# Two output banks with a longer scheduled lag, a second transpose bank in the drain, and every sixth gate multiplication on GpSimd, in a scan followed by a mixture of adapters

## Chip, cores, metric

One core of a Trainium2 chip runs the whole program. The metric is device microseconds (us) of one execution, lower is better. "PE" is the matmul engine TensorE, "PEld" its weight loads.

## The reference, cut to what matters

```python
# a, b: (8, 6400, 128) float32;  w_gate (128, 8), A (8, 128, 16), B (8, 16, 128)
for t in range(S):                      # linear recurrence along 6400 steps
    h = a[:, t] * h + b[:, t]
    x[:, t] = h
logits = x @ w_gate                     # 51200 rows, 8 experts
# the two largest logits of a row, softmax over these two -> weights g
# delta = sum over these two e of g_e * (x @ A[e]) @ B[e]
out = x + delta
```

The kernel works on 100 tiles of 512 rows. It computes Z = x @ [A0 .. A7] (128 columns) for all experts, multiplies by the gate g (zero for the six experts not chosen), and multiplies by the stacked B.

## The kernel before

Each tile w passes these steps. Names are those of the program, and the same names stand in the profile.

| step | engine | what |
|---|---|---|
| A, B | PE | float32 transposes of the rows of a and b into pA and pB |
| aev | ScalarE | copy pA to a_st |
| scan | VectorE | the recurrence, from a_st and pB to xT (f16) |
| L | PE | logits into pL, 8 columns wide |
| lev ... sig | ScalarE, VectorE, GpSimd | gating, once for a group of four tiles |
| Z | PE | x @ A into pZ |
| mul | VectorE | zw = Z * gate |
| T | PE | transposes of zw into pT |
| tev | ScalarE | copy pT to zwT |
| R | PE | delta (zwT @ B) and residual (x through an identity matrix), both added up in pO |
| oev | ScalarE | copy pO to outt; then a store |

PSUM has eight banks in this kernel, each used whole or in part by one buffer:

```python
pA = sb(nc.psum_tensor("pA", [128, UT], F32))
pB = [sb(nc.psum_tensor(f"pB{i}", [128, UT], F32)) for i in range(2)]
pL = sb(nc.psum_tensor("pL", [128, 512], F32))
pZ = [sb(nc.psum_tensor(f"pZ{i}", [128, UT], F32)) for i in range(NZ)]   # NZ = 2
pT = sb(nc.psum_tensor("pT", [128, 1024], F16))
pO = [sb(nc.psum_tensor(f"pO{i}", [128, UT], F32)) for i in range(NO)]   # NO = 1
```

The order of each engine's queue is made when the program is built. A list scheduler simulates all engines with estimated durations and gives the free engine the ready operation with the smallest key (third argument). The engines then work through these fixed queues with semaphores.

```python
add(f"Z{w}", "pe", w + 5, 230.0, emit, [f"scan{w}", f"mul{w - NZ}", "cst"])
...
add(f"T{w}", "pe", w + 6, 225.0, emit, [f"mul{w}", f"tev{w - 1}", "idh"])
...
for i in range(Q):                       # delta and residual, interleaved
    c = o[:, i * 128 : (i + 1) * 128]
    h.matmul(c, zwT[w % 2][:, i * 128 : (i + 1) * 128], Bcat_h, start=True, stop=False)
    last = h.matmul(c, x_block(w, i), ident_h[:, :], start=False, stop=True)
...
add(f"R{w}", "pe", w + 6.5, 455.0, emit, [f"tev{w}", f"oev{w - NO}"])
```

A key of w + 6 means: T of tile w goes ahead of A of tile w + 6 if both are ready. So the keys say how many tiles the second half of the work lags behind the first. (UT is 512 rows, Q is 4 blocks of 128.)

## Time and profile before

| | before |
|---|---|
| time, median of the 4 runs beside the changed kernel's | 222.56 us (221.56 to 223.5) |
| span of the profiled run | 221.2 us |
| period of a tile in the body (31st to 91st a_st copy, 61.59 to 178.73 us) | 1.952 us |
| last a_st copy starts | 196.30 us |
| output evacuations still to come then | 12 |
| last output evacuation starts | 218.00 us |

From the page of the profile: busy time by engine, the GB/s moved in 40 slices, and the chain of work that ended last, by engine.

```profile
PE 204.4 (92%) x2800; PEld 195.6 (88%) x2800; DVE 191.5 (87%) x261; ACT 174.2 (79%) x356; POOL 90.5 (41%) x195
...
GB/s 183 379 387 387 385 385 388 385 402 402 398 402 398 398 400 399 399 399 397 399 397 398 402 398 402 397 397 402 398 398 401 395 400 400 320 180 134 156 131 153
...
PE 82%; DVE 7%; ACT 3%; DMA 2%; issue 2%; POOL 1%; SPq 1%; DVEq 0%; ACTq 0%; POOLq 0%
```

Read the GB/s row as three stages: a start, a body near 400 GB/s, and six slices of 5.5 us at the end in which little but stores is left and little moves. Those last slices are the drain. The table by stretches says who is busy in body and drain (columns: stretch, its length, busy time of each engine, granted clock, DMA share, GB/s):

```profile
core 0: us, PE busy (x) PEld busy (x) DVE busy (x) ACT busy (x) POOL busy (x), PEclk, DMA share, GB/s
60.00:180.00 120.00, 120.00 (x1729) 119.08 (x1727) 116.49 (x158) 105.63 (x216) 53.97 (x108) 1.00 1.05 399
200.00:212.00 12.00, 7.50 (x112) 6.36 (x112) 5.43 (x12) 7.58 (x20) 5.61 (x20) 1.00 0.40 147
```

One tile of PE's queue in the body, from the timeline (start, duration, engine, line, what). Durations overlap because matmuls are pipelined; read start to start:

```profile
187.22 0.39 PE L472 MATMUL pT<-ident_h,zw 128*128 128x128 f16 x4
187.44 0.27 PE L338 MATMUL pL<-cst_h,xT 128*128 128x8 f16 x4
187.60 0.41 PE L449 MATMUL pZ<-cst_h,xT 128*128 128x128 f16 x4
187.85 0.61 PE L282 MATMUL pA<-ident_f,a_in 128*128 128x128 f32 x4
188.29 0.60 PE L282 MATMUL pB<-ident_f,b_in 128*128 128x128 f32 x4
188.73 0.22 PE L493 MATMUL pO<-cst_h,zwT 128*128 128x128 f16 x1
```

T 0.22, logits 0.16, Z 0.25, A 0.44, B 0.44, and eight delta and residual matmuls until the next T at 189.18: 1.96 us.

And the chain of waits in the drain (start, duration, what), for one tile:

```profile
211.81 0.59 ACT outt L505
212.40 0.50 ACT zwT L483
...
212.94 0.23 PE pO L493
...
213.60 0.35 ACT outt L505
```

Evacuate pO, evacuate pT, delta and residual, evacuate pO again: a loop through one bank of each kind, 1.79 us here. Z, T and R take PE 0.93 us a tile at the pace of the body; for the rest it waits.

### The profile page before, as it was taken

What the parts mean: (1) busy time and instruction counts of PE and PEld (TensorE: products, weight loads), DVE (VectorE), ACT (ScalarE), POOL (GpSimd) and SP (SyncE); (2) the same over time, 40 slices, a digit from 0 to 9 for tenths busy, and PEclk for the clock granted to TensorE, in tenths of its full rate; (3) what the DMA queues carried; (4) which work ended last, traced back from release to release, by engine and by line L of the source; (5) the groups of instructions that cost most, each with busy time, mean ns of one, the idle gap of its engine ahead of it and who ended that gap; (6) DMA issues with size and microseconds to landing.
All of it is one profiled execution on the core that took longest, in us unless ns stands there. A gap on an engine that the chain in (4) does not pass through costs nothing.

```text
span 221.2 us, 6969 instructions
## 1 busy us (share of the span) xinstructions
PE 204.4 (92%) x2800; PEld 195.6 (88%) x2800; DVE 191.5 (87%) x261; ACT 174.2 (79%) x356; POOL 90.5 (41%) x195
## 2 busy tenths in 40 slices
PE   3889999999999999999999999999999999987552
PEld 2767889999999999999999999999999999985441
DVE  0499999999999999999999999999999999994320
ACT  3245589888889888888888898888899888876653
POOL 1016425435353543534445253443535435357400
PEclk9999999999999999999999999999999999999985
DMA  7999999999999999999999999999999999843434
GB/s 183 379 387 387 385 385 388 385 402 402 398 402 398 398 400 399 399 399 397 399 397 398 402 398 402 397 397 402 398 398 401 395 400 400 320 180 134 156 131 153
DMA packets 42208, 79.23 MB, mean 358 GB/s; under 512 B 3648, under 2 KB 3776, under 8 KB 42176
## 3 DMA queue, kind: packets, MB, share of 16 engines
q1 hardware_dynamic: 40848, 78.65, 94.3%
q8 instruction: 22, 0.36, 0.7%
q10 hardware_dynamic: 1328, 0.14, 0.5%
q14 instruction: 10, 0.08, 0.1%
HBM read 52.56 MB, written 26.21 MB: 356 GB/s over the span
## 4 chain that ended last, share of the span: by engine, by line
PE 82%; DVE 7%; ACT 3%; DMA 2%; issue 2%; POOL 1%; SPq 1%; DVEq 0%; ACTq 0%; POOLq 0%
PE pA L282 19%; PE pB L282 18%; PE pZ L449 12%; PE pO L493 10%; PE pO L494 10%; PE pT L472 9%; DVE xT L313 5%; PE pL L338 5%; DMA b_in<-in_b_dram 2%; DVE zw L465 2%; ACT outt L505 2%; ACT zwT L483 1%; SPq L266 1%; POOL pn L417 0%; ACT a_st L296 0%
## 5 line engine op out<-in xcount | busy, mean ns | idle before, releaser
L313 DVE TENSOR_TENSOR_SCAN xT<-a_st,xT,pB 128x512 f16<-128x512 f32 x96 | 120.0, 1250 | 3.4 <-PE pB L282 1.6
L505 ACT COPY outt<-pO 128x512 f32<-128x512 f32 x100 | 58.9, 589 | 28.3 <-PE pO L494 27.5
L465 DVE TENSOR_TENSOR zw<-pZ,g 128x512 f16<-128x512 f32 x100 | 67.3, 674 | 10.9 <-PE pT L472 5.8
L296 ACT COPY a_st<-pA 128x512 f32<-128x512 f32 x100 | 59.3, 593 | 12.8 <-PE pA L282 8.3
L282 PE MATMUL pA<-ident_f,a_in 128*128 128x128 f32 x400 | 63.1, 281 | 3.8 <-DMA a_in<-in_a_dram 3.8
L282 PE MATMUL pB<-ident_f,b_in 128*128 128x128 f32 x400 | 61.2, 277 | 0.1
L493 PE MATMUL pO<-cst_h,zwT 128*128 128x128 f16 x400 | 56.2, 221 | 4.8 <-ACT zwT L483 4.8
L483 ACT COPY zwT<-pT 128x512 f16<-128x512 f16 x100 | 58.9, 589 | 0.4 <-PE pT L472 0.4
L494 PE MATMUL pO<-ident_h,xT 128*128 128x128 f16 x400 | 56.2, 221 | 0.0
L282 PEld LDWEIGHTS pA<-ident_f,a_in 128*128 128x128 f32 x400 | 43.0, 143 | 5.3 <-DMA a_in<-in_a_dram 4.2
L282 PEld LDWEIGHTS pB<-ident_f,b_in 128*128 128x128 f32 x400 | 46.9, 142 | 0.9 <-DMA b_in<-in_b_dram 0.9
L494 PEld LDWEIGHTS pO<-ident_h,xT 128*128 128x128 f16 x400 | 45.1, 114 | 1.0
L493 PEld LDWEIGHTS pO<-cst_h,zwT 128*128 128x128 f16 x400 | 39.2, 99 | 6.3 <-ACT zwT L483 6.1
L449 PE MATMUL pZ<-cst_h,xT 128*128 128x128 f16 x400 | 40.7, 225 | 3.6 <-DVE zw L465 3.5
L472 PE MATMUL pT<-ident_h,zw 128*128 128x128 f16 x400 | 39.0, 220 | 0.0
L449 PEld LDWEIGHTS pZ<-cst_h,xT 128*128 128x128 f16 x400 | 26.4, 117 | 5.0 <-DVE zw L465 4.5
L338 PE MATMUL pL<-cst_h,xT 128*128 128x8 f16 x400 | 27.4, 174 | 1.3 <-DVE xT L313 0.9
L472 PEld LDWEIGHTS pT<-ident_h,zw 128*128 128x128 f16 x400 | 26.7, 98 | 0.0
L338 PEld LDWEIGHTS pL<-cst_h,xT 128*128 128x128 f16 x400 | 23.5, 117 | 3.6 <-DVE xT L313 3.4
L377 POOL TENSOR_TENSOR d_0<-Lg,m_0 128x128 f32<-128x128 f32 (+2 forms) x14 | 5.4, 388 | 36.2 <-DVE m_0 L369 36.2
L409 POOL TENSOR_TENSOR d_0<-Lg,m_0 128x128 f32<-128x128 f32 (+2 forms) x14 | 5.5, 390 | 25.7 <-DVE m_0 L401 25.7
L409 POOL TENSOR_TENSOR d_1<-Lg,m_1 128x128 f32<-128x128 f32 (+1 forms) x13 | 5.2, 397 | 23.7 <-DVE m_1 L401 23.2
(29 smaller groups left out, 114.5 us busy)
## 6 DMA issues: line engine op xcount, KB each, us to landing
a_in<-in_a_dram SPq DMA_DIRECT2D x49, 512.0 KB, 11.2
b_in<-in_b_dram SPq DMA_DIRECT2D x49, 512.0 KB, 11.3
out_dram<-outt SPq DMA_DIRECT2D x49, 512.0 KB, 11.1
a_in<-in_a_dram SPq DMA_DIRECT2D x2, 256.0 KB, 3.6
b_in<-in_b_dram SPq DMA_DIRECT2D x2, 256.0 KB, 4.3
out_dram<-outt SPq DMA_DIRECT2D x2, 256.0 KB, 2.0
cst_f<-in_moe_A_dram ACTq DMA_DIRECT2D x1, 64.0 KB, 4.0
cst_f<-in_moe_B_dram ACTq DMA_DIRECT2D x1, 64.0 KB, 4.4
```

The lines of the kernel that those rows point to most:

```text
L282: last = h.transpose(view[:, i, :], ring[:, w % RING, i * 128 : (i + 1) * 128], ident_f[:, :])
L296: lambda h: h.copy(a_st[w % 2][:, :], pA[:, :]),
L313: last = h.tensor_tensor_scan(out=xT[:, x0 + lo : x0 + hi], data0=a_st[w % 2][:, lo:hi], data1=pB[w % 2][:, lo:hi], initial=init, op0=ALU. ...
L338: last = h.matmul(pL[:, c : c + E], x_block(w, i), wg_h)
L409: lambda h: h.tensor_tensor(out=v(d2[s]), in0=v(Lg[s]), in1=bc(m2[s]), op=ALU.subtract),
L449: last = h.matmul(pZ[w % NZ][:, i * 128 : (i + 1) * 128], x_block(w, i), Acat_h)
L465: lambda h: h.tensor_tensor(out=oview, in0=zview, in1=gview, op=ALU.mult),
L472: last = h.transpose(pT[:, i * 128 : (i + 1) * 128], zw[w % 2][:, i, :], ident_h[:, :])
L483: lambda h: h.copy(zwT[w % 2][:, :], pT[:, 0:UT]),
L493: h.matmul(c, zwT[w % 2][:, i * 128 : (i + 1) * 128], Bcat_h, start=True, stop=False)
L494: last = h.matmul(c, x_block(w, i), ident_h[:, :], start=False, stop=True)
L505: lambda h: h.copy(outt[:, w % NOUT, :], pO[w % NO][:, :]),
```

## The change

Its intent is to shorten the drain by giving it more banks and a second evacuating engine, and to relieve VectorE in the body. The core of the diff, with cuts marked (most comments after # are this text's):

```diff
-    NZ, NO = 2, 1
+    NZ, NO = 2, 2
+    TAIL = 10
+    KZ, KT, KR, KD = 8, 8.2, 8.6, 8.0        # keys of Z, T, residual, delta
+    PM = 6
...
-    groups = cut((), 4, (2, 1, 1))
+    groups = cut((1, 1, 2), 4, ())           # small groups first, none at the end
...
-        pL = sb(nc.psum_tensor("pL", [128, 512], F32))
+        pTL = sb(nc.psum_tensor("pTL", [128, 512], F32))   # T and logits share a bank
+        pT = pTL[:, 0 : UT // 2].bitcast(F16)
+        pL = pTL[:, UT // 2 : UT // 2 + GB * E]
...
+        # scheduler: an operation on a shared bank also waits for the other
+        # engine's last operation there
...
+            ge = "dve" if k == len(groups) - 1 else "pool"   # last gating on VectorE, key -6
...
+        def on_pool(w):
+            return w % PM == 3 and 8 < w < NU - 16            # tiles 9, 15 ... 81
...              # for these: ScalarE copies pZ to z_sb, GpSimd multiplies from z_sb
+        def spare(w):
+            return w >= NU - TAIL and w % 2 == 1              # T into pA, free by then
...
         def delta(w):                                        # residual first, then delta
+            add(f"R{w}", "pe", w + KR, 226.0, emit_x, [f"scan{w}", f"oev{w - NO}", "idh"])
+            add(f"D{w}", "pe", w + KD, 226.0, emit_d, [f"R{w}", f"tev{w}", "cst"])
...
         def o_evac(w):
+            oe = "dve" if w >= NU - TAIL and w % 2 == 0 else "act"
```

More of the change, by code (lines that the diff above doesn't have):

```diff
@@ L10, with __init__ @@
 AX = mybir.AxisListType
-PRINT = False
 class _Op:
-    def __init__(self, name, eng, key, busy, lat, emit, deps, dma):
+    def __init__(self, name, eng, key, busy, lat, emit, deps, dma, bank):
         self.name = name
@@ L27, in __init__ @@
         self.dma = dma
+        self.bank = bank
         self.signal = False
@@ L38, in __init__, with add @@
         self.order = {e: [] for e in sems}
-    def add(self, name, eng, key, busy, lat, emit, deps=(), dma=None):
-        self.ops[name] = _Op(name, eng, key, busy, lat, emit, list(deps), dma)
+    def add(self, name, eng, key, busy, lat, emit, deps=(), dma=None, bank=None):
+        self.ops[name] = _Op(name, eng, key, busy, lat, emit, list(deps), dma, bank)
     def schedule(self, dma_rate):
@@ L55, in schedule @@
         link = 0.0
+        bank = {}
         for op in ops.values():
@@ L62, in schedule @@
             for e, c in cand.items():
-                if c:
-                    t = max(free[e], min(r for r, _ in c))
-                    if best is None or t < best[0]:
-                        best = (t, e)
-            t, e = best
-            pick = min((x for x in cand[e] if x[0] <= t), key=lambda x: (x[1].key, x[0]))
+                for x in c:
+                    other = [end[o.name] for o in bank.get(x[1].bank, {}).values() if o.eng != e]
+                    t = max([free[e], x[0]] + other)
+                    if best is None or (t, x[1].key) < best[:2]:
+                        best = (t, x[1].key, e, x)
+            t, _, e, pick = best
             cand[e].remove(pick)
             op = pick[1]
+            if op.bank:
+                held = bank.setdefault(op.bank, {})
+                op.deps += [o for o in held.values() if o.eng != e]
+                held[e] = op
             self.order[e].append(op)
@@ L184, in bass_associative_scan_2x2__then__mixture_of_adapters_kernel @@
         zwT = [sb(nc.sbuf_tensor(f"zwT{i}", [128, UT], F16)) for i in range(2)]
+        z_sb = sb(nc.sbuf_tensor("z_sb", [128, UT], F32))
         outt = sb(nc.sbuf_tensor("outt", [128, NOUT, UT], F32))
@@ L201, in bass_associative_scan_2x2__then__mixture_of_adapters_kernel @@
         pB = [sb(nc.psum_tensor(f"pB{i}", [128, UT], F32)) for i in range(2)]
-        pL = sb(nc.psum_tensor("pL", [128, 512], F32))
+        pTL = sb(nc.psum_tensor("pTL", [128, 512], F32))
+        pT = pTL[:, 0 : UT // 2].bitcast(F16)
+        pL = pTL[:, UT // 2 : UT // 2 + GB * E]
         pZ = [sb(nc.psum_tensor(f"pZ{i}", [128, UT], F32)) for i in range(NZ)]
-        pT = sb(nc.psum_tensor("pT", [128, 1024], F16))
         pO = [sb(nc.psum_tensor(f"pO{i}", [128, UT], F32)) for i in range(NO)]
@@ L211, in bass_associative_scan_2x2__then__mixture_of_adapters_kernel, with add @@
         plan = _Plan(sems)
-        def add(name, eng, key, busy, emit, deps=(), dma=None):
+        def add(name, eng, key, busy, emit, deps=(), dma=None, bank=None):
             lat = {"pe": 190.0, "dve": 120.0, "act": 150.0, "pool": 100.0, "sp": 100.0}[eng]
-            plan.add(name, eng, key, busy, lat, emit, deps, dma)
+            plan.add(name, eng, key, busy, lat, emit, deps, dma, bank)
         def add_dma(name, eng, key, emit, slot, nbytes, deps=()):
@@ L339, in emit @@
                 return last
-            add(f"L{w}", "pe", w + 1, 140.0, emit, [f"scan{w}", f"lev{k - 1}", "cst"])
+            add(f"L{w}", "pe", w + 1, 140.0, emit, [f"scan{w}", f"lev{k - 1}", "cst"], bank="TL")
         def gating(k):
@@ L346, in gating, with cost @@
             s = k % 2
-            key = u0 + n + 0.5
-            fixed = 60.0 + 75.0 * (4 - n)
+            key = u0 + n + (0.5 if k < len(groups) - 1 else -6)
+            ge = "dve" if k == len(groups) - 1 else "pool"
+            def cost(t):
+                return 200.0 if ge == "dve" else t
             def v(t):
@@ L362, in gating @@
                 [f"L{w}" for w in range(u0, u0 + n)] + [f"p4_{k - 2}", f"p3_{k - 2}", f"p6_{k - 2}"],
+                bank="TL",
             )
@@ L373, in gating @@
                 f"p1_{k}",
-                "pool",
+                ge,
                 key,
-                410.0,
+                cost(410.0),
                 lambda h: h.tensor_tensor(out=v(d1[s]), in0=v(Lg[s]), in1=bc(m1[s]), op=ALU.subtract),
@@ L381, in gating @@
                 f"p2_{k}",
-                "pool",
+                ge,
                 key,
-                650.0,
+                cost(650.0),
                 lambda h: h.tensor_scalar(v(pn[s]), v(d1[s]), 0.0, -1.0e30, ALU.is_ge, ALU.mult),
@@ L389, in gating @@
                 f"p3_{k}",
-                "pool",
+                ge,
                 key,
-                460.0,
+                cost(460.0),
                 lambda h: h.tensor_tensor(out=v(L2[s]), in0=v(Lg[s]), in1=v(pn[s]), op=ALU.add),
@@ L405, in gating @@
                 f"p4_{k}",
-                "pool",
+                ge,
                 key,
-                410.0,
+                cost(410.0),
                 lambda h: h.tensor_tensor(out=v(d2[s]), in0=v(Lg[s]), in1=bc(m2[s]), op=ALU.subtract),
@@ L413, in gating @@
                 f"p5_{k}",
-                "pool",
+                ge,
                 key,
-                650.0,
+                cost(650.0),
                 lambda h: h.tensor_scalar(v(pn[s]), v(d2[s]), 0.0, -1.0e30, ALU.is_lt, ALU.mult),
@@ L421, in gating @@
                 f"p6_{k}",
-                "pool",
+                ge,
                 key,
-                460.0,
+                cost(460.0),
                 lambda h: h.tensor_tensor(out=v(d1[s]), in0=v(d1[s]), in1=v(d2[s]), op=ALU.add),
@@ L429, in gating @@
                 f"p7_{k}",
-                "pool",
+                ge,
                 key,
-                460.0,
+                cost(460.0),
                 lambda h: h.tensor_tensor(out=v(um[s]), in0=v(d1[s]), in1=v(pn[s]), op=ALU.add),
@@ L450, in emit @@
                 return last
-            add(f"Z{w}", "pe", w + 5, 230.0, emit, [f"scan{w}", f"mul{w - NZ}", "cst"])
+            add(f"Z{w}", "pe", w + KZ, 230.0, emit, [f"scan{w}", f"mul{w - NZ}", f"zev{w - NZ}", "cst"])
+        def on_pool(w):
+            return w % PM == 3 and 8 < w < NU - 16
         def z_mul(w):
@@ L457, in z_mul, with t_dst, t_bank @@
             gview = g[k % 3][:, o : o + Q, :].unsqueeze(3).broadcast_to([128, Q, E, R])
-            zview = pZ[w % NZ][:, :].rearrange("p (q e r) -> p q e r", q=Q, e=E, r=R)
             oview = zw[w % 2][:, :, :].rearrange("p q (e r) -> p q e r", e=E)
+            deps = [f"sig{k}", f"T{w - 2}"]
+            if on_pool(w):
+                src = z_sb
+                add(
+                    f"zev{w}",
+                    "act",
+                    w + 5.5,
+                    480.0,
+                    lambda h: h.copy(z_sb[:, :], pZ[w % NZ][:, :]),
+                    [f"Z{w}", f"mul{w - PM}"],
+                )
+                eng, busy, deps = "pool", 1200.0, deps + [f"zev{w}"]
+            else:
+                src = pZ[w % NZ]
+                eng, busy, deps = "dve", 600.0, deps + [f"Z{w}"]
+            zview = src[:, :].rearrange("p (q e r) -> p q e r", q=Q, e=E, r=R)
             add(
                 f"mul{w}",
-                "dve",
+                eng,
                 w + 5.5,
-                600.0,
+                busy,
                 lambda h: h.tensor_tensor(out=oview, in0=zview, in1=gview, op=ALU.mult),
-                [f"Z{w}", f"sig{k}", f"T{w - 2}"],
+                deps,
             )
+        def spare(w):
+            return w >= NU - TAIL and w % 2 == 1
+        def t_dst(w):
+            return pA[:, 0 : UT // 2].bitcast(F16) if spare(w) else pT
+        def t_bank(w):
+            return "A" if spare(w) else "TL"
         def zw_tr(w):
@@ L471, in emit @@
                 for i in range(Q):
-                    last = h.transpose(pT[:, i * 128 : (i + 1) * 128], zw[w % 2][:, i, :], ident_h[:, :])
+                    last = h.transpose(t_dst(w)[:, i * 128 : (i + 1) * 128], zw[w % 2][:, i, :], ident_h[:, :])
                 return last
-            add(f"T{w}", "pe", w + 6, 225.0, emit, [f"mul{w}", f"tev{w - 1}", "idh"])
+            add(
+                f"T{w}",
+                "pe",
+                w + KT,
+                225.0,
+                emit,
+                [f"mul{w}", "idh", f"tev{w - 2 if w > NU - TAIL else w - 1}"] + [f"aev{NU - 1}"] * spare(w),
+                bank=t_bank(w),
+            )
         def t_evac(w):
@@ L482, in t_evac, with emit_x, emit_d @@
                 480.0,
-                lambda h: h.copy(zwT[w % 2][:, :], pT[:, 0:UT]),
-                [f"T{w}", f"R{w - 2}"],
+                lambda h: h.copy(zwT[w % 2][:, :], t_dst(w)),
+                [f"T{w}", f"D{w - 2}"],
+                bank=t_bank(w),
             )
         def delta(w):
-            o = pO[w % NO]
-            def emit(h):
+            def emit_x(h):
                 for i in range(Q):
-                    c = o[:, i * 128 : (i + 1) * 128]
-                    h.matmul(c, zwT[w % 2][:, i * 128 : (i + 1) * 128], Bcat_h, start=True, stop=False)
-                    last = h.matmul(c, x_block(w, i), ident_h[:, :], start=False, stop=True)
-                return last
-            add(f"R{w}", "pe", w + 6.5, 455.0, emit, [f"tev{w}", f"oev{w - NO}"])
+                    last = h.matmul(
+                        pO[w % NO][:, i * 128 : (i + 1) * 128],
+                        x_block(w, i),
+                        ident_h[:, :],
+                        start=i == 0,
+                        stop=False,
+                        skip_group_check=True,
+                    )
+                return last
+            def emit_d(h):
+                for i in range(Q):
+                    last = h.matmul(
+                        pO[w % NO][:, i * 128 : (i + 1) * 128],
+                        zwT[w % 2][:, i * 128 : (i + 1) * 128],
+                        Bcat_h,
+                        start=False,
+                        stop=True,
+                        skip_group_check=True,
+                    )
+                return last
+            add(f"R{w}", "pe", w + KR, 226.0, emit_x, [f"scan{w}", f"oev{w - NO}", "idh"])
+            add(f"D{w}", "pe", w + KD, 226.0, emit_d, [f"R{w}", f"tev{w}", "cst"])
         def o_evac(w):
+            oe = "dve" if w >= NU - TAIL and w % 2 == 0 else "act"
             add(
                 f"oev{w}",
-                "act",
+                oe,
                 w + 6.5,
-                480.0,
-                lambda h: h.copy(outt[:, w % NOUT, :], pO[w % NO][:, :]),
-                [f"R{w}", f"st{store_of.get(w - NOUT)}"],
+                600.0 if oe == "dve" else 480.0,
+                lambda h: (h.tensor_copy if oe == "dve" else h.copy)(outt[:, w % NOUT, :], pO[w % NO][:, :]),
+                [f"D{w}", f"st{store_of.get(w - NOUT)}"],
             )
@@ L545, in bass_associative_scan_2x2__then__mixture_of_adapters_kernel @@
         plan.schedule(390.0)
-        print("plan", plan.span) if PRINT else None
         block = sb(nc.Block())
```

## The prediction

> **What bounds the kernel now.** TensorE, until the last input tile; a chain of round trips after that. In the table by stretches, PE is busy 40.00 of 40 us from 60 to 180 us at clock 1.00. In the timeline each 512-row tile takes 1.95 us there: A and B transposes 0.44-0.49 us each, delta and residual 0.45, T 0.22, Z 0.22-0.28, logits 0.12, back to back. VectorE is nearly as full (38.8 of 40 us; scan 1.19 us issue to issue, multiplication 0.58), and DMA moves about 400 GB/s from 30 to 190 us; 78.65 MB at that rate is 197 us, so a much faster body is not to be had. PE has holes before 22 us (the first transposes of zw start at 23 us).
>
> The last A/B transposes are issued at 196 us. After that 12 output evacuations remain and end at 218.6 us. In this drain the timeline shows 1.87 us a tile, though PE needs only 0.93 (Z, T, delta, residual). The loop is on ScalarE: evacuate pO (0.48 issue to issue), evacuate pT (0.59), then PE's delta (0.45 and a wait), and only then pO again; with one pO and one pT nothing overlaps. The chain of waits ends in just these lines.
>
> **What the change does.**
> 1. Two pO banks, residual matmuls ahead of the delta, a second transpose bank (pA, free then) and half of the output evacuations on VectorE for the last 10 tiles. The loop breaks. Per tile then: PE 0.93, VectorE 0.58 + 0.3, ScalarE 0.48 + 0.24. I estimate 0.95 to 1.1 us a tile instead of 1.87: 12 tiles save 9 to 11 us. This is all critical.
> 2. Small first groups let draining start earlier and fill PE's holes before 22 us: 0 to 3 us. The last group is a full four tiles, but its gating goes to VectorE with first priority: about 3 us, hidden behind tiles not yet drained.
> 3. 13 of 100 multiplications (tiles 9, 15 ... 81) go to GpSimd. VectorE loses 13 x 0.58 = 7.5 us, ScalarE gains 13 copies (6 to 8 us). Neither is the limit in the body. GpSimd's tensor_tensor takes 297 ns for 64 and 410 ns for 128 elements, so about 1.1 us (estimate) for 512; the Trainium skill's "GPSIMD Engine Reference", Specifications, says it has no PSUM access, hence the copy. Worth about 0 (-1 to +2 us).
> 4. T and logits now share a bank with ordered access; the skill's "PSUM — Partial Sum Buffer", Terms, forbids PE and another engine in one bank at once, so logits must wait for ScalarE's evacuation (0.59 us) and the reverse. It fits in 1.95 us, but may leave PE holes: 0 to 4 us lost.
>
> PE's work is unchanged. Sum: 221.7 - 10 - 1.5 + 1 = about 211 us; floor about 205 (3.8 until the first matmul, 2 slow first tiles, 195, and 4 for the last evacuation and store).
>
> **Predicted: 210.5 us, 206 to 216 in 8 of 10.** Faster by over 2%: 0.89; within 2%: 0.09; slower: 0.02.
>
> **What would show it.** Body still 1.93 to 1.97 us a tile with PE full. About 12 evacuations after the last A/B transposes, spaced 0.95 to 1.1 us, alternating ScalarE and VectorE; last evacuation near 207-208 us. GpSimd multiplications near 1.1 us; VectorE down to about 36.5 of 40 us in the body, with no gain in period. DMA rate unchanged in the body, higher in the drain.
>
> **What would make it wrong.** PE waits at the shared bank in every tile (0.05 us each is 5 us); GpSimd multiplications far over 1.2 us that hold back Z two tiles later; the last group's gating coming late, so that the drain waits for it; a longer backlog at the last A/B transposes.

## More of the kernel before

In the body PE is busy without a hole as the profile draws it (the ends of matmuls are modelled, so a wait of some hundredths of a us does not show here; the third set comes back to this), and VectorE (DVE) nearly so; in the drain no engine is busy for more than two thirds of the time. The weight loads (PEld) are as full as the matmuls, 119.08 of 120 us.

In the last two tiles of this profile (213.6 to 218.0 us) the granted clock was 0.50, delta and residual matmuls started 0.11 us apart instead of 0.06, and a tile took 2.20 us.

## The result, and the profile after

The changed kernel took 212.91 us (median of 4, 212.89 to 213.47) against 222.56 us (221.56 to 223.5) beside it. The ratio is 0.957, interval 0.952 to 0.963. A ratio is the mean time of one kernel's fast runs over that of the other's of the same rounds, so it is not quite the ratio of the medians.

The spans of the two profiled runs, 221.2 and 211.1 us, differ by 10.1 us. The starts of the copies on the timeline say where:

| stage | before, us | after, us | gain |
|---|---|---|---|
| start to 7th a_st copy | 15.46 | 15.20 | 0.26 |
| 7th to 31st a_st copy | 46.13 | 45.21 | 0.92 |
| 31st to 91st a_st copy (period of a tile) | 117.14 (1.952) | 115.45 (1.924) | 1.69 |
| 91st to last a_st copy | 17.57 | 16.85 | 0.72 |
| last a_st copy to last output evacuation (evacuations in it) | 21.70 (12) | 15.11 (13) | 6.59 |
| from there to the end | 3.2 | 3.3 | -0.1 |

The same parts of the page as before:

```profile
PE 201.8 (96%) x2800; PEld 193.4 (92%) x2800; DVE 190.7 (90%) x260; ACT 174.1 (82%) x364; POOL 100.2 (47%) x201
...
GB/s 185 381 388 385 386 386 387 391 393 397 397 400 392 402 397 398 401 398 401 397 397 399 398 401 399 396 401 399 402 399 396 402 395 399 399 392 278 200 243 257
...
PE 89%; DVE 4%; DMA 2%; ACT 1%; issue 1%; SPq 0%; DVEq 0%
```

The slow slices at the end are now four of 5.3 us, at 200 to 278 GB/s. The same two stages by engine (columns as above):

```profile
60.00:180.00 120.00, 119.99 (x1750) 119.09 (x1749) 114.43 (x150) 108.99 (x230) 66.98 (x123) 1.00 1.05 398
...
200.00:208.00 8.00, 6.98 (x101) 5.80 (x100) 6.35 (x11) 5.95 (x12) 0.00 (x0) 1.00 0.62 230
```

PE's share in the drain rose from 63% to 87%. In the body PE was full and is full; VectorE lost 2 of 120 us.

One tile of PE's queue in the body:

```profile
122.21 0.39 PE L550 MATMUL pO<-cst_h,zwT 128*128 128x128 f16 x4
122.43 0.39 PE L511 MATMUL pTL<-ident_h,zw 128*128 128x128 f16 x4
122.65 0.27 PE L346 MATMUL pTL<-cst_h,xT 128*128 128x8 f16 x4
122.78 0.39 PE L461 MATMUL pZ<-cst_h,xT 128*128 128x128 f16 x4
123.01 0.61 PE L290 MATMUL pA<-ident_f,a_in 128*128 128x128 f32 x4
123.45 0.39 PE L538 MATMUL pO<-ident_h,xT 128*128 128x128 f16 x4
123.67 0.61 PE L290 MATMUL pB<-ident_f,b_in 128*128 128x128 f32 x4
```

From 122.21 to the next delta at 124.12: 1.91 us. Logits take 0.13 and Z 0.23, against 0.16 and 0.25 in the tile shown of before. The work is the same, so something in the order or the waits changed.

The end of the drain on ScalarE, then on VectorE (timeline of one engine each; the bracket is the idle time before an instruction and what ended it):

```profile
203.66 0.59 ACT L570 COPY outt<-pO 128x512 f32<-128x512 f32 x1
204.62 0.58 ACT L530 COPY zwT<-pA 128x512 f16<-128x512 f16 x1 [0.36 <-PE pA L511]
205.29 0.58 ACT L530 COPY zwT<-pTL 128x512 f16<-128x512 f16 x1
205.77 0.59 ACT L570 COPY outt<-pO 128x512 f32<-128x512 f32 x1
206.67 0.58 ACT L530 COPY zwT<-pA 128x512 f16<-128x512 f16 x1 [0.31 <-PE pA L511]
207.82 0.58 ACT L570 COPY outt<-pO 128x512 f32<-128x512 f32 x1 [0.56 <-PE pO L550]
```

```profile
204.54 0.68 DVE L570 COPY outt<-pO 128x512 f32<-128x512 f32 x1
205.14 0.68 DVE L495 TENSOR_TENSOR zw<-pZ,g 128x512 f16<-128x512 f32 x1
206.45 0.69 DVE L570 COPY outt<-pO 128x512 f32<-128x512 f32 x1 [0.63 <-PE pO L550]
```

The evacuations alternate: 203.66, 204.54, 205.77, 206.45, 207.82. The last ten (from 198.87 us on, the tiles that may use the second transpose bank) lie 0.99 us apart on average. The three intervals before them (193.60, 195.24, 197.05, 198.87) are 1.76 us each on average. The granted clock was 1.00 throughout this drain. In e4 below, whose drain has the loop of the kernel before, it stayed at 1.00 too and the last tiles took 1.78 us: so about 0.8 of the 6.6 us that the two profiled drains differ by is the lower clock in the last two tiles of the one before.

The GpSimd multiplications, as a group of instructions (count, busy us, mean ns of one, idle time before):

```profile
L495 POOL TENSOR_TENSOR zw<-z_sb,g 128x512 f16<-128x512 f32 x13 | 13.8, 1061 | 4.3 <-PE pTL L346 3.3 <-PE pA L290 1.0
```

### The profile page after: what moved, and what is told of

It is laid out like the page before. It is cut to its first block, busy times and chain, and to the rows that moved or that the text cites. A ratio compares the mean times of both kernels' runs of the same rounds, so it can differ in the third digit from the quotient of the medians.

```text
span 211.1 us, 7035 instructions
## 1 busy us (share of the span) xinstructions
PE 201.8 (96%) x2800; PEld 193.4 (92%) x2800; DVE 190.7 (90%) x260; ACT 174.1 (82%) x364; POOL 100.2 (47%) x201
## 4 chain that ended last, share of the span: by engine, by line
PE 89%; DVE 4%; DMA 2%; ACT 1%; issue 1%; SPq 0%; DVEq 0%
PE pA L290 20%; PE pB L290 20%; PE pO L550 11%; PE pZ L461 11%; PE pO L538 11%; PE pTL L511 10%; PE pTL L346 5%; DVE xT L321 4%; DMA a_in<-in_a_dram 2%; ACT outt L570 1%; ACT zwT L530 1%; PE pA L511 0%; SPq L274 0%; DVE m_1 L413 0%; DVE m_0 L381 0%
## 5 line engine op out<-in xcount | busy, mean ns | idle before, releaser
L530 ACT COPY zwT<-pTL 128x512 f16<-128x512 f16 x95 | 56.6, 596 | 2.2 <-PE pTL L511 1.6
L550 PE MATMUL pO<-cst_h,zwT 128*128 128x128 f16 x400 | 38.6, 219 | 0.9 <-ACT zwT L530 0.7
L538 PE MATMUL pO<-ident_h,xT 128*128 128x128 f16 x400 | 39.0, 221 | 0.4 <-ACT outt L570 0.2
L511 PE MATMUL pTL<-ident_h,zw 128*128 128x128 f16 x380 | 36.8, 219 | 0.0
L538 PEld LDWEIGHTS pO<-ident_h,xT 128*128 128x128 f16 x400 | 32.3, 114 | 1.6 <-ACT outt L570 1.2
L550 PEld LDWEIGHTS pO<-cst_h,zwT 128*128 128x128 f16 x400 | 29.4, 98 | 3.0 <-PE pO L538 1.4
L346 PE MATMUL pTL<-cst_h,xT 128*128 128x8 f16 x400 | 27.3, 174 | 0.9 <-DVE xT L321 0.6
L346 PEld LDWEIGHTS pTL<-cst_h,xT 128*128 128x128 f16 x400 | 23.7, 116 | 2.8 <-DVE xT L321 2.4
L511 PEld LDWEIGHTS pTL<-ident_h,zw 128*128 128x128 f16 x380 | 25.2, 98 | 0.1
L495 POOL TENSOR_TENSOR zw<-z_sb,g 128x512 f16<-128x512 f32 x13 | 13.8, 1061 | 4.3 <-PE pTL L346 3.3
```

The lines of the kernel that those rows point to most:

```text
L346: last = h.matmul(pL[:, c : c + E], x_block(w, i), wg_h)
L495: lambda h: h.tensor_tensor(out=oview, in0=zview, in1=gview, op=ALU.mult),
L511: last = h.transpose(t_dst(w)[:, i * 128 : (i + 1) * 128], zw[w % 2][:, i, :], ident_h[:, :])
L530: lambda h: h.copy(zwT[w % 2][:, :], t_dst(w)),
L538: last = h.matmul(pO[w % NO][:, i * 128 : (i + 1) * 128], x_block(w, i), ident_h[:, :], start=i == 0, stop=False, skip_group_check=True,)
L550: last = h.matmul(pO[w % NO][:, i * 128 : (i + 1) * 128], zwT[w % 2][:, i * 128 : (i + 1) * 128], Bcat_h, start=False, stop=True, skip_gro ...
```

## The experiments

Twelve kernels were run, all correct, in four sets. Each set shared its chip with runs of the kernel before, so ratios to the kernel before are compared. "Period" is from the 31st to the 91st a_st copy; "drain" is from the start of the last a_st copy to that of the last output evacuation. The scheduler orders all queues anew in each run, so an edit can change PE's order as well as what it names.

| run | time, us | ratio to before (interval) | period, us | drain, us |
|---|---|---|---|---|
| before | 222.56 | 1 | 1.952 | 21.70 |
| the change | 212.91 | 0.957 (0.952 to 0.963) | 1.924 | 15.11 |
| e1_no_pool | 214.27 | 0.961 (0.957 to 0.965) | 1.925 | 15.09 |
| e2_no_split | 214.02 | 0.960 (0.955 to 0.965) | 1.921 | 15.66 |
| e3_one_pO | 220.77 | 0.992 (0.987 to 0.997) | 1.947 | 21.49 |
| e4_before_pool | 224.09 | 1.005 (1.000 to 1.009) | 1.944 | 22.77 |
| e5_one_pT | 217.53 | 0.980 (0.978 to 0.983) | 1.924 | 19.64 |
| e6_oev_act | 213.43 | 0.961 (0.959 to 0.963) | 1.924 | 14.84 |
| e7_gate_pool | 213.04 | 0.960 (0.958 to 0.962) | 1.925 | 14.29 |
| e8_two_pO_only | 236.83 | 1.066 (1.064 to 1.068) | 2.136 | 21.55 |
| e9_logits_last | 215.90 | 0.969 (0.965 to 0.973) | 1.954 | 15.34 |
| e10_two_pO_lag | 220.61 | 0.990 (0.985 to 0.995) | 1.909 | 24.01 |
| e11_mix | 215.70 | 0.968 (0.964 to 0.971) | 1.920 | 17.89 |
| e12_gate_pool_lz | 212.78 | 0.958 (0.954 to 0.962) | 1.920 | 14.29 |

The period and the drain come from one profile each. They are steadier than the times: in the change, e5, e6 and e7, whose program is the same until the drain, the 7th a_st copy began at 15.20, 14.94, 15.91 and 16.78 us, but the 91st came 160.66, 160.69, 160.68 and 160.70 us after it. So what differs between these executions is mostly the start. The drains have one more difference: in the profiles of before, e3, e8, e10 and e11 the granted clock fell to about half for the last 2 to 5 us, in the others not; where the loop can be compared the last tiles are 0.2 to 0.4 us longer each, so differences of under 1 us between these drains and others are not read.

### First set: what made the body faster, and is the single pO bank the drain's loop?

**e1_no_pool**, on the changed kernel:

```diff
-            return w % PM == 3 and 8 < w < NU - 16
+            return False
```

> The changed kernel without the GpSimd multiplications and their ScalarE copies (all 100 back on VectorE). Theory A (the body's gain, 1.952 to 1.924 us a tile, comes from PE's order: residual apart from the delta, logits before Z more often): the period stays within 0.01 us of 1.924 and the time within 0.8 us of 212.9. Theory B (it comes from VectorE's relief of 0.1 us a tile, which ends small PE waits for the scan and the multiplication): the period goes back to 1.94-1.95 us and the time to 214.5-216.

Measured: period 1.925 us, time 214.27. The body keeps its gain though VectorE is busier in it than in the kernel before (118.00 of 120 us between 60 and 180 us, against 116.49). Theory B falls. The time lies between what the two theories said, and the ratio is 0.003 above the change's (0.7 us), with intervals that overlap: that the GpSimd part is worth anything is not shown. Its profile has 1.949 us a tile from the 91st to the last a_st copy, against 1.872 in the change, so relief of VectorE may help there; one profile does not settle it.

**e2_no_split**, on the changed kernel: residual and delta interleaved in one operation with the delta's key.

```diff
...
-            add(f"R{w}", "pe", w + KR, 226.0, emit_x, [f"scan{w}", f"oev{w - NO}", "idh"])
-            add(f"D{w}", "pe", w + KD, 226.0, emit_d, [f"R{w}", f"tev{w}", "cst"])
+            add(f"D{w}", "pe", w + KD, 455.0, emit, [f"scan{w}", f"oev{w - NO}", "idh", f"tev{w}", "cst"])
```

> The changed kernel with residual and delta matmuls issued together and interleaved again, at the delta's place. Theory A: the period goes back to about 1.95 us and the time to 215 or more. Theory B: the period stays near 1.924 us; the drain loses at most 1 us because the residual no longer runs ahead, so 212.9 to 214.

Measured: period 1.921 us, drain 15.66 us, time 214.02. The split is not what made the body faster, so Theory A falls as far as it named the split.

**e3_one_pO**, on the changed kernel:

```diff
-    NZ, NO = 2, 2
+    NZ, NO = 2, 1
```

> The changed kernel with one pO bank. If the single pO bank closes the loop of the old drain (evacuate pO, then delta, then evacuate again), the last ten tiles go from 1.0 back to 1.4-1.9 us each and the time to 217-220. If the second transpose bank and the VectorE evacuations carry the drain, it loses under 2 us: below 215.

Measured: 220.77 us (0.8 above the range expected), drain 21.49 us, and the period went back to 1.947. Nearly the whole gain is gone. PE's queue says where most of the period went: A now stands right after the logits in 55 of 62 tiles (12 of 62 in the change; the third set shows what this costs). The chain of waits in its drain:

```profile
206.94 0.59 ACT outt L570
...
207.59 0.43 PE pO L538 x4
...
208.06 0.41 PE pO L550 x4
...
208.50 0.70 DVE outt L570
```

The loop is evacuation, residual, delta, evacuation, through the one bank: 1.56 us, although the transposes have two banks and the evacuations two engines.

**e4_before_pool**: the kernel before with the change's GpSimd multiplications and their copies alone.

> The kernel before with the GpSimd multiplications alone. Theory A: period stays 1.95 us and the time within 1 us of the kernel before (ratio 0.995 to 1.005). Theory B: period 1.925 us, time down by 2 to 3 us (ratio 0.987 to 0.991).

Measured: period 1.944 us, ratio 1.005 (1.000 to 1.009). GpSimd alone gives nothing, perhaps costs half a per cent. It is not a clean test of relief, though: PE's queue came out with A right after the logits in 59 of 61 tiles (30 of 61 before), which costs time, while a wait of Z (third set) went away.

### Second set: which parts carry the drain?

**e5_one_pT**, on the changed kernel:

```diff
         def spare(w):
-            return w >= NU - TAIL and w % 2 == 1
+            return False
...
-                [f"mul{w}", "idh", f"tev{w - 2 if w > NU - TAIL else w - 1}"] + ...
+                [f"mul{w}", "idh", f"tev{w - 1}"] + ...
```

> The changed kernel without the second transpose bank in the drain. Theory C (the drain is now bound by VectorE, which is busy without a hole from 189 to 205 us): one transpose bank with its loop of about 1.1 us (T 0.22, evacuation 0.6, two waits of 0.15 each) is hardly longer than the 1.0 us a tile now, so 212.9 to 214. Rival D (the transpose bank carries the drain): over 215.

Measured: 217.53 us, ratio 0.980, drain 19.64 us. Theory C fell here: the transpose bank is worth 4.5 us of drain. The arithmetic of a 1.1 us loop had left out that the queues are in order. The chain of waits shows what really follows what:

```profile
206.05 0.59 ACT outt L570
206.63 0.50 ACT zwT L530
...
207.26 0.40 PE pO L550 x4
...
207.69 0.70 DVE outt L570
```

Evacuate pO, and behind it in ScalarE's queue evacuate pT; then the delta; then the next evacuation: 1.64 us. ScalarE's two copies run one after the other in the loop, as in the kernel before.

**e6_oev_act**, on the changed kernel:

```diff
-            oe = "dve" if w >= NU - TAIL and w % 2 == 0 else "act"
+            oe = "act"
```

> The changed kernel with all output evacuations on ScalarE. Theory C: VectorE is relieved of 5 x 0.6 = 3 us in the drain, ScalarE has 2 x 0.49 us a tile, so it is no slower: 211.5 to 213.2. Rival D (sharing the evacuations is what shortened the drain): 215 or more.

Measured: 213.43 us, 0.2 us above the range that Theory C gave; drain 14.84 us, 0.3 shorter than the change's. VectorE's share of the evacuations is not needed: with two banks of each kind ScalarE alone keeps up.

**e7_gate_pool**, on the changed kernel:

```diff
-            ge = "dve" if k == len(groups) - 1 else "pool"
+            ge = "pool"
```

> The changed kernel with the last group's gating on GpSimd. Theory C: VectorE is relieved of about 2 us, but the gate of the last four tiles comes about 1 to 2 us later (GpSimd 3.5 us for what VectorE does in 2 us); the two cancel: 212.5 to 214. Rival D (early gating is what the drain needs): 215 or more.

Measured: 213.04 us, drain 14.29 us. The last gating on VectorE is not needed either. e6 and e7 agree with a VectorE that is loaded in the drain (it is busy 13.46 of the drain's 15.1 us, PE 13.74), but the ratios of both lie within the change's interval, so no gain is shown.

**e8_two_pO_only**: the kernel before with only the two pO banks. T and logits share a bank for it, with the scheduler's ordering of the shared bank; keys (Z 5, T 6, R 6.5), groups, gating, evacuations, interleaving and multiplications are as before.

> The kernel before with only two pO banks (T and logits share a bank for that; keys, groups, gating, evacuations, residual and multiplications as before). If the second pO bank is the change's main part: period 1.92-1.93 us, drain about 1.1-1.3 us a tile, time 213 to 216.5. If it helps only together with the other parts: period 1.95 and over 218.

Measured: 236.83 us, ratio 1.066, slower than the kernel before (222.15 us in this set) by 14.7 us. The period is 2.136 us, which neither expectation had. ScalarE's timeline in its body shows the wait:

```profile
123.14 0.59 ACT L553 COPY outt<-pO 128x512 f32<-128x512 f32 x1 [0.33 <-PE pO L541]
123.70 0.59 ACT L530 COPY zwT<-pTL 128x512 f16<-128x512 f16 x1
124.20 0.59 ACT L304 COPY a_st<-pA 128x512 f32<-128x512 f32 x1
```

The a_st copy stands behind an evacuation that waits for the delta of the same round. The scan (at 124.82) waits for a_st, PE's B transposes wait for an earlier scan to leave pB (they start 0.75 us after A here, 0.44 without a wait; the list of waits has 20 such waits of PE for the scan), and the delta comes after B. Two suspects were left: the old keys with their short lag, and the shared bank.

### Third set: order, lag, and an attempt

For the order of PE's queue, take the mean time from the first matmul of a group to the first of the next group, from the timelines between 60 and 180 us, by what stood before it:

| group | before | the change | e9_logits_last | e10_two_pO_lag |
|---|---|---|---|---|
| A after Z | 0.443 | 0.443 | none | 0.442 |
| A after logits | 0.470 | 0.471 | 0.471 | 0.470 |
| Z after T | 0.237 | 0.226 | 0.228 | 0.223 |
| Z after logits | 0.250 | 0.229 | none | 0.228 |
| logits after T | 0.158 | 0.134 | once | 0.129 |
| logits after Z | 0.130 | 0.127 | 0.130 | 0.126 |
| tiles with A right after logits | 30 of 61 | 12 of 62 | 61 of 61 | 8 of 63 |

A group of float32 transposes costs 0.03 us more right after the 8-column logits. It is not a matter of A: in e1, where B sometimes follows logits, B took 0.471 there and 0.443 after Z, and in e4 A followed logits in nearly every tile and took 0.471. The extra lies between the first and the second of the four matmuls: 143 ns after logits, 115 after Z, and 109 between the later ones.

The other difference in the table, at logits and Z, is a wait. From the timeline before, the end of a VectorE multiplication and the first weight load of the Z behind it:

```profile
100.99 0.67 DVE L465 TENSOR_TENSOR zw<-pZ,g 128x512 f16<-128x512 f32 x1
101.71 0.26 PEld L449 LDWEIGHTS pZ<-cst_h,xT 128*128 128x128 f16 x4
```

Z of tile w writes the pZ bank that the multiplication of tile w - 2 reads, and waits for it. In 58 of 62 tiles of the kernel before, Z's first weight load starts late, within 56 ns after the end of such a multiplication; in the change in 3 of 62, in e9 in 11 of 62, in e1, e4 and e10 in none. Weighted by how often each neighbour occurs, the table and the same means for the other groups give, from before to the change, -0.012 us a tile at logits and -0.015 at Z, -0.008 at A (fewer after logits), +0.007 at B (0.437 right after A before, 0.444 after the residual now), and nothing at T, delta and residual. So this wait accounts for nearly all of the body's 0.028 us.

**e9_logits_last**, on the changed kernel, after scheduling:

```diff
+        seq = self.order["pe"]
+        for i in range(len(seq) - 1):
+            if seq[i].name[0] == "L" and seq[i + 1].name[0] == "Z":
+                seq[i], seq[i + 1] = seq[i + 1], seq[i]
```

> The changed kernel, with each adjacent pair of logits and Z in PE's queue exchanged where logits stood first, so that the 8-column logits always stand directly before the A transposes. Theory E (the body's gain is an order of PE's queue that the two pO banks allow: A's float32 transposes take 0.47 us a tile after logits, 0.44 after Z): in the 50 of 62 tiles affected the tile costs about 0.03 us more, the period goes from 1.924 to 1.945-1.955 and the time up by 1.5 to 2.5 us. If order is not it: period and time unchanged within 0.005 us and 0.5 us.

Measured: period 1.954 us, ratio 0.969 against 0.957, which is 0.0116 of 222.5, or 2.6 us. The order costs what Theory E said, in the time a little more. As an account of the gain over the kernel before, Theory E fails: there only 30 of 61 tiles had A after logits, which is 0.008 of the 0.028 us, and B gives that back. One tile of its PE queue:

```profile
123.47 0.41 PE L465 MATMUL pZ<-cst_h,xT 128*128 128x128 f16 x4
123.72 0.27 PE L350 MATMUL pTL<-cst_h,xT 128*128 128x8 f16 x4
123.85 0.63 PE L294 MATMUL pA<-ident_f,a_in 128*128 128x128 f32 x4
124.32 0.39 PE L542 MATMUL pO<-ident_h,xT 128*128 128x128 f16 x4
```

A takes 124.32 - 123.85 = 0.47 us here, and 123.45 - 123.01 = 0.44 in the tile of the changed kernel above.

**e10_two_pO_lag**, on e8:

```diff
-    KZ, KT, KR, KD = 5, 6, 6.5, 6.5
+    KZ, KT, KR, KD = 8, 8.2, 8.6, 8.0
```

> As the fourth run of the second set (the kernel before with only two pO banks), but with the new keys: Z, T and delta wait for 8 tiles more of A and B instead of 5 to 6.5. If the short lag made that run slow (ScalarE's evacuation of pO waits for the delta and holds up the a_st copy behind it, so the scan and PE's B transposes come late): period back to 1.92-1.93 us and time 215 to 219, with the drain still at 1.6-1.9 us a tile. If the shared T and logits bank made it slow: period stays over 2.05 us and the time over 230.

Measured: period 1.909 us, time 220.61, drain 24.01 us for 13 evacuations, 1.87 us apart in its middle, as in the kernel before. The time is 1.6 us above the expected range, with a drain at the upper end of what was expected for each tile. So the shared bank was innocent and the old keys were what slowed e8. That it was their short lag, and not the order among Z, T and delta that they also set, is argued from e8's timeline and not tested. This kernel has the fastest body of all, with all multiplications on VectorE:

```profile
60.00:180.00 120.00, 120.00 (x1762) 119.38 (x1760) 118.66 (x161) 105.95 (x220) 55.91 (x112) 1.00 1.05 399
```

It also shows that the second pO bank alone does not shorten the drain: with pT single and ScalarE making all copies, the loop is the old one.

**e11_mix**, on the changed kernel: last gating on GpSimd, the pairs of Z and logits exchanged the other way (logits first), and TAIL = 14.

> Attempt at a faster version: the changed kernel with the last gating on GpSimd (its drain was 0.8 us shorter from the last a_st copy to the last evacuation), logits always ahead of Z where they are neighbours (0.03 us for 12 of 62 tiles, 0.5 us), and the drain's second transpose bank and VectorE evacuations from tile 86 instead of 90 (first four drain tiles 1.75 us apart now, 1.1-1.4 hoped for). Hoped: 210 to 212. If VectorE or the order of the queues holds the early drain: 212.5 to 214.

Measured: 215.70 us, drain 17.89 us: worse. VectorE now evacuates outputs where it should still scan, the last scan starts at 197.24 us (193.53 in the change), its logits follow, and the last gate is ready only after 204.5 us. These two lines of its timeline show VectorE idle for 1.70 us waiting for that gate:

```profile
204.48 0.31 ACT L458 ACTIVATE g<-um 128x128 f32<-128x128 f32 x1 [0.97 <-POOL um L449]
204.82 2.10 DVE L499 TENSOR_TENSOR zw<-pZ,g 128x512 f16<-128x512 f32 x3 [1.70 <-ACT g L458]
```

### Fourth set

**e12_gate_pool_lz**: e11 with TAIL = 10 again.

> The changed kernel with the last group's gating on GpSimd and logits always ahead of Z, the drain otherwise as in the change. From the profiles: 12 of 62 tiles in the body 0.03 us shorter (period 1.919, 0.5 us in all), drain 0.8 us shorter: 211.3 to 212.5, ratio 0.951 to 0.956. If the gains are not additive or are below what the start of the run varies by: 212.5 to 213.5, ratio 0.956 to 0.961.

Measured: ratio 0.958 (0.954 to 0.962), the same as the change. Its profile does have the period (1.920) and the drain (14.29) hoped for, but the timed runs do not show a gain. No version that beats the change was found.

## Why the prediction was right

The time (210.5 predicted, 206 to 216; 212.91 measured) was right, but partly because two misses cancelled: of the sum 221.7 - 10 - 1.5 + 1, the drain gave 6.6 us instead of 10 (0.8 of it the clock), and the body gave 2.4 us where 1 was to be lost.

1. **"What bounds the kernel now" was right in the main**: PE in the body (with the short wait of point 6), a loop of round trips in the drain. e3, e5 and e10 show the loop: take away the second bank of either kind and the drain goes back to 19.6 to 24.0 us. The Trainium skill ("Perfetto Trace Analysis", Optimizing Tensor Performance, Matmuls) advises to rotate matmul groups through PSUM banks so that evacuation overlaps the next group. This case agrees and adds a condition: all banks of the loop have to be doubled. With pO doubled and new keys but nothing else of the change for the drain it took 24.0 us (e10), with all of the change but the second pO bank 21.5 (e3), with all of it but the second transpose bank 19.6 (e5), with everything 15.1.

2. **"12 tiles save 9 to 11 us" was mis-sized.** The rate (0.95 to 1.1 us a tile) was right for the last ten tiles, which run 0.99 us apart. But the evacuations on VectorE start only at tile 90 and the second transpose bank at tile 91, and there were 13 evacuations left: the intervals from tile 87 to 90 still took 1.76 us each. The term should have been 3 x 1.76 + 9 x 0.99 = 14.2 us from first to last evacuation, which is what the timeline has (193.60 to 207.82), against 20.8 before: 6.6 us. e11 shows that TAIL cannot simply be raised: VectorE is still scanning then.

3. **"Half of the output evacuations on VectorE" and the last gating on VectorE** were counted as parts of the gain. e6 and e7 do without one of them each: the drain is no longer (14.84 and 14.29 against 15.11 us), and the ratios (0.961 and 0.960) lie within the change's interval.

4. **"Small first groups ... 0 to 3 us"**: the change gains 0.92 us between the 7th and the 31st a_st copy, within the range, but not for the reason given. e10 has the old groups and needs 45.39 us there, e4 too and needs 45.26, against 45.21 in the change and 46.13 in the kernel before. So the small groups are not needed for it. The wait of Z from point 6 is a candidate: between these two copies it stands in 14 of 20 tiles before, in none of 19 in the change, in 4 of 19 in e10 and 6 of 18 in e4. No run tests it.

5. **GpSimd "about 0 (-1 to +2 us)" was right.** One multiplication took 1.061 us (estimate 1.1), VectorE's busy time in the body fell by 2 of 120 us, and nothing came of it in the period: e1 without it has the same one. e4 with it alone is no faster, but with another order of PE's queue. The Trainium skill ("GPSIMD Engine Reference", Engine selection) says about 2 times slower than VectorE for two inputs; here 1.061 against 0.669 us, 1.6 times.

6. **"Body still 1.93 to 1.97 us a tile" was wrong**, and so was the fear behind "0 to 4 us lost" at the shared bank. The period fell to 1.924. "PE's work is unchanged" was true in instructions and wrong in time. In the kernel before, Z waited in 58 of 62 tiles for VectorE's multiplication two tiles back to leave its pZ bank, though the profile shows PE as 100% busy; in the change it does in 3 of 62. With what this costs at the logits before Z it is nearly all of the 0.028 us. It is not a matter of VectorE's load, since e1 and e10 have no such wait with a fuller VectorE, nor of the second pO bank or the split, since e3 has it in 1 of 61 tiles and e2 in 2 of 63; when Z comes after its multiplication is set by the order of the queues. Second, logits right before float32 transposes cost 0.03 us. The runs with A after logits in nearly every tile (e3, e4, e9) have periods of 1.944 to 1.954 without the wait of Z or with little of it; the change has A there in 12 of 62 (1.924), e10 in 8 of 63 (1.909).

7. **The shared bank did no harm, but the way to it could have.** e8 has the two pO banks with the old keys and loses 14.7 us; e10 with the new keys loses nothing in the body. The keys of about eight tiles in the diff look like tuning numbers, and in these two runs they decide whether the second bank costs 14.7 us or nothing. The skill ("PSUM — Partial Sum Buffer", PSUM bank collisions raise a hardware error) has two engines at once in one bank, on the same 32 partitions, as an error; all runs here kept that order, so none shows what happens without it.

Open: whether the kernel before, with one pO bank, would gain from a better order of PE's queue alone; which of the parts is needed to remove the wait of Z, since each of several runs lacks it; where the 0.92 us before the 31st copy come from; and why a float32 group is slower after logits.

## What to carry to other kernels

When a drain runs at a fraction of every engine, write down the loop of buffers that closes it and double every bank in that loop, not the one that seems worst; then check from which tile on the doubling holds. In a body that looks full on one engine, relief for another engine was worth nothing here, but the order of the full engine's own queue was worth a per cent and a half. A busy share of 100% hid waits of 0.03 us a tile: compare start-to-start times of each group by what stands before it, and look at what ended just before a group that starts late. And when a resource is added, the priorities that suited the old resources may turn it into a loss.

## What the Trainium skill lacked or had wrong

- "TensorE: Matmul & The Clock Gate", Back-to-back issue gap, gives about 81 ns as the sustained spacing of pairs of weight load and matmul with 128 columns. Here such pairs in f16 run in the body 0.223 us for four, 56 ns each, which the page has as its isolated figure.
- No page read has the cost of a narrow matmul for what follows it: four float32 transposes took 0.470 us right after the 8-column logits and 0.442 to 0.445 after 128-column matmuls (before, the change, e9, e10).
- No page read says how much the start of a program varies: with the same program until the drain, the 7th a_st copy began between 14.94 and 16.78 us (the change, e5, e6, e7).
- "GPSIMD Engine Reference", Engine selection, has about 2 times for a two-input operation; with VectorE reading one operand from PSUM and writing f16, the ratio was 1.6 (1.061 to 0.669 us).
